# Attention maxima without two small VectorE operations, and every head's first weight tile in float32

## The chip, the cores and the metric

The kernel runs on one core of one Trainium2 chip. The metric is the device time of one execution in microseconds (us). Shown are the median of three runs, and one profiled execution from which all rows come.

## The reference, cut to what matters

Causal attention with a decay bias, then a mixture of experts, then a gated convolution block. Only attention is touched by the change.

```python
def _attn_ref(q, k, v, s):            # q, k, v: 4 x 8 x 576 x 64; s: 4 x 8 x 576
    scores = scale * np.matmul(q, k.transpose(0, 1, 3, 2))
    cum = np.cumsum(np.maximum(s, 0.0), axis=-1)
    bias = -(cum[:, :, :, None] - cum[:, :, None, :])
    scores = np.where(causal, -1e9, scores + np.minimum(bias, 0.0))
    scores = scores - np.max(scores, axis=-1, keepdims=True)
    attn = np.exp(scores)
    attn = attn / (np.sum(attn, axis=-1, keepdims=True) + 1e-09)
    return np.matmul(attn, v)
```

## The kernel before

**Units and steps.** The 32 pairs of batch and head are worked in 8 units of 4 heads. A sequence of 576 is four blocks of 128 positions and a tail of 64; the tails of two heads share one tile. A unit has 14 steps, one score tile each: per pair of heads (0,0), (0,1), (0,2), (1,0), (1,1), (1,2), (1,3), as (head, g). Tile g = 0 has the 512 scores of the head's key block 0 with its four query blocks; the others have the rest of the triangle and the tails. All engines work in the order in which the program is written, so the order is set by the loop over steps and by tables of step numbers (`PAR`).

**One step** (the loop at the end of `attention`) writes, in this order: the maxima's reductions that the step before left (`am`); the planned work of the step; the score products of this tile (`scores`, L443, L446, L471, into `z`, three PSUM buffers); up to two pieces of the *next* unit's maxima products (`stage_a`, L335, into `za`, two PSUM buffers), whose reductions go on VectorE at the start of the next step; the exponentials of the tile one step back (`weights`, ScalarE); `rest` of the tile two steps back; and, when a head's last tile is four steps back, its products with v (`values`, L515), then the normalization.

**Maxima.** The row maxima of a unit must be known before its scores are used, since they enter as a row of the score product. `stage_a` makes 14 pieces. Pieces 0 to 10 are the blocks of 128 queries. `last(r)`, r = 0 and 1, has the tails of two heads against 512 keys, and `lastd` the tails against the tails, with the mask. Each piece ends in a VectorE `tensor_reduce` (L338) into columns of `mx` (float32, 128 x 20): 0 to 15 the blocks, 16 and 17 `last`, 18 and 19 `lastd`. Then `max_cols`, two small VectorE operations: the larger of columns 16, 17 and 18, 19 (L398), and all 18 columns scaled by 2^-12 into float16 (L401). `max_turn` transposes these on TensorE by a product with a float16 identity (L411, into `mt`), `max_out` copies the result to SBUF on ScalarE (L416), and `max_row` writes it into the unit's key tile by DMA. For unit 0 the same is done in three parts (L404, L406).

**Precision of the weights.** The products with v need more than float16. `mode(x)` gives each tile (unit, head, g) with g < 3 a letter from `PAR['m']`, a string of three letters a head:

- `a`: ScalarE writes the exponential twice, as float16 `phi` (L487) and as float32 in place in PSUM (L488); VectorE subtracts the two into float16 `plo` (L499). The score buffer is free after that. `values` makes three float16 products of 65 columns with v's two halves.
- `b`: as `a`, but the float32 copy goes to SBUF (`p`) and GpSimd subtracts (units 0 to 2 use `a` in its place).
- `f`: ScalarE writes the exponential once, as float32 in SBUF (L482), and the score buffer is free. `values` makes one float32 product with the float32 `v0`, which the trace shows as two matmul rows.

Before, the string is `baa baa faa aaa`: only head 2's first tile is in float32. A head has four products with its tile g = 0, one for each query block.

**Behind attention** come the routing (a chain of small operations), the experts, fed by weight loads through a ring of buffers, and the convolution block.

Of the kernel before, what the change touches and what calls it, by code (L numbers as in the profile page):

```python
# [10 lines left out]
F16 = mybir.dt.float16  # L11
I32 = mybir.dt.int32
AF = mybir.ActivationFunctionType
ALU = mybir.AluOpType
# [6 lines left out]
NT = B * S  # L21
# [17 lines left out]
def bc(ap, shape):  # L39
    return ap.to_broadcast(shape)  # L40


class Keep:
# [45 lines left out]
           'pb': 0.377,  # L89
           'c2': 1.0,  # L90
           'pt': 1.003,
           'mct': 1.1,
           'sv0': 1.103,
           'T10': 1.106,
           'mtt': 1.203,
# [8 lines left out]
           'z': 5.0,  # L104
           'lv1': 5.997},
 'r': {'cut': 12, 'w1': 6, 'w2': 8, 'w3': 22},
 'm': 'baabaafaaaaa'}


BEGIN = ([(0, 0), (0, 1), (1, 0), (1, 1), (0, 2), (1, 2), (1, 3)],  # L110
# [3 lines left out]
def attention(tc, ctx, q, k, v, s, xd, rt, hook):  # L114
# [22 lines left out]
    hlp = pool("hl", 1, **right).tile([128, 2, 16, 2, 64], F16, name="h")  # L137
    cum = pool("cum", 1, on=tctx, side="right")

    zero = const.tile([128, 256], F16, name="zero")  # L140
    ident = const.tile([128, 128], F32, name="ident")
    id16 = const.tile([128, 128], F16, name="id16")
    identm = const.tile([128, 128], F16, name="identm")
# [7 lines left out]
    U = {}  # L151
# [171 lines left out]
    mxs = {}  # L323

    def stage_a(u, halves=False):

        mx = mxs[u] = wk.tile([128, 20], F32, name="mx")
        def mcol(i, hs):
            c = 8 * (i % 2) + i // 2 + 2 * hs[0]
            return mx[:, c:c + 2 * len(hs) - 1:2]  # L330

        t, tt = U[u, 1][0:70], T1[0:70]

        def mm(out, l, r, start, stop=False):
            PE.matmul(out, lhsT=l, rhs=r, start=start, stop=stop, skip_group_check=True)  # L335

        def rowmax(out, z, m):
            return lambda: V.tensor_reduce(out, z.rearrange("p (e c) -> p e c", e=m), axis=AX.X, op=ALU.max)  # L338

        def piece(i, hs):  # L340

            n, m = 128 * i + 128, len(hs)
            z = aps.tile([128, 512], F32, name="za")
            for x, h in enumerate(hs):
                y, l = z[:, x * n:x * n + n], block(t, 1, h, i)
                k = whole(t, 0, h)
                if i == 1:
                    mm(y, l, k[:, :, 0:128], x == 0)
                elif i == 3:
                    mm(y, l, k, x == 0)  # L350
                else:
                    mm(y[:, 0:128 * i // 2 + 128], l, k[:, 0, 0:128 * i // 2 + 128], x == 0)
                    if i == 2:
                        mm(y[:, 256:384], l, block(t, 0, h, 1), False)
            for x, h in enumerate(hs):
                c = x * n + (0, 128, 128, 384)[i]
                mm(z[:, c:c + 128], identm, triq, False, True)
            return rowmax(mcol(i, hs), z[:, 0:m * n], m)

        def last(r):  # L360
            z = aps.tile([128, 512], F32, name="za")
            for e in range(2):
                mm(z[64 * e:64 * e + 64], tail(tt, 1, u, 2 * r + e), whole(t, 0, 2 * r + e), True, True)
            return rowmax(mx[:, 16 + r:17 + r], z, 1)

        def lastd(rs):
            z = aps.tile([128, 512], F32, name="za")
            for x, r in enumerate(rs):
                for e in range(2):
                    mm(z[64 * e:64 * e + 64, 64 * x:64 * x + 64], tail(tt, 1, u, 2 * r + e), tail(tt, 0, u, 2 * r + e), x == 0)  # L370
            for x in range(len(rs)):
                mm(z[:, 64 * x:64 * x + 64], identm, tailq, False, True)
            m = len(rs)
            return rowmax(mx[:, 18 + rs[0]:18 + rs[0] + m], z[:, 0:64 * m], m)

        P = []
        if halves:
            for h in (0, 2):
                P += [lambda h=h: piece(0, (h, h + 1)), lambda h=h: piece(1, (h, h + 1))]
                P += [lambda h=h, e=e, i=i: piece(i, (h + e,)) for i in (2, 3) for e in range(2)]  # L380
        else:
            P.append(lambda: piece(0, (0, 1, 2, 3)))
            P += [lambda h=h: piece(1, (h, h + 1)) for h in (0, 2)]
            P += [lambda h=h, i=i: piece(i, (h,)) for i in (2, 3) for h in range(4)]
        P += [lambda r=r: last(r) for r in range(2)] + [lambda: lastd((0, 1))]
        return P


    def key(hs):
        return hs.start if hs else 16  # L390
# [1 line left out]
    def span(hs, tails):  # L392
        return slice(0 if hs else 16, 18 if tails else 8)

    def max_cols(u, hs=slice(0, 4), tails=True):
        mx = mxs[u]
        if tails:
            V.tensor_tensor(mx[:, 16:18], mx[:, 16:18], mx[:, 18:20], op=ALU.max)  # L398
        m = U[u, "16", key(hs)] = wk.tile([128, 18], F16, name="m16")
        if hs == slice(0, 4):  # L400
            V.tensor_scalar(m, mx[:, 0:18], 2.0 ** -12, None, op0=ALU.mult)  # L401
        elif hs:
            i = lambda x: x[:, 0:16].rearrange("p (e h c) -> p e h c", e=2, c=2)[:, :, hs]
            V.tensor_scalar(m[:, 0:8].rearrange("p (e h c) -> p e h c", e=2, c=2), i(mx), 2.0 ** -12, None, op0=ALU.mult)  # L404
        else:
            V.tensor_scalar(m[:, 16:18], mx[:, 16:18], 2.0 ** -12, None, op0=ALU.mult)  # L406

    def max_turn(u, hs=slice(0, 4), tails=True):
        t = U[u, "mt"] = mps.tile([128, 512], F32, name="mt")
        r = span(hs, tails)  # L410
        PE.matmul(t[0:r.stop - r.start, 0:128], lhsT=U[u, "16", key(hs)][:, 0:r.stop - r.start] if key(hs) != 16 else U[u, "16", 16][:, 16:18], rhs=id16, start=True, stop=True, skip_group_check=True)  # L411

    def max_out(u, hs=slice(0, 4), tails=True):
        n = span(hs, tails).stop - span(hs, tails).start
        mr = U[u, "mr", key(hs)] = wk.tile([18, 128], F16, name="mr")
        A.activation(mr[0:n], U[u, "mt"][0:n, 0:128], AF.Copy)  # L416

    def max_row(u, hs=slice(0, 4), tails=True):
        n = 0
# [193 lines left out]
    def plan(t, f):  # L613
        todo.setdefault(math.floor(t), []).append((t, len(todo), f))
# [8 lines left out]
    def begin_a():  # L623
        P0.extend(stage_a(0, True))
        for f in P0[0:6]:
            f()()
        max_cols(0, first, False)

    def second_a():
        for f in P0[6:12]:  # L630
            f()()
        max_cols(0, second, False)

    begin_tasks = dict(
        lk1=lambda: load(1, "k"), lq1=lambda: load(1, "q"), st=lambda: (split_tail("k"), split_tail("q")), tt=turn_tail, ct=copy_tail,
# [1 line left out]
        pa=begin_a, sk1=lambda: split_qk(1, "k"), sq1=lambda: split_qk(1, "q"), mt0a=lambda: max_turn(0, first, False), mo0a=lambda: max_out(0, first, False),  # L637
        mr0a=lambda: max_row(0, first, False), T10=lambda: turn(1, 0), T11=lambda: turn(1, 1), x1=lambda: extra(1),
        pb=second_a, sv0=lambda: split_v(0), lk2=lambda: load(2, "k"), lq2=lambda: load(2, "q"),
        pt=lambda: [P0[12 + i]()() for i in range(3)], mct=lambda: max_cols(0, None), mtt=lambda: max_turn(0, None), mot=lambda: max_out(0, None), mrt=lambda: max_row(0, None),  # L640
        mtb=lambda: max_turn(0, second, False), mob=lambda: max_out(0, second, False), mrb=lambda: max_row(0, second, False),
        z=lambda: Q.dma_start(xd[NT:NT + 128].rearrange("p (j c) -> p j c", c=256), bc(zero[:, None], [128, 4, 256])))
    for n, t in PAR["start"].items():
        plan(t, begin_tasks[n])
    seq = []
# [7 lines left out]
    for u in range(1, NU):  # L653
# [13 lines left out]
        plan(t0 + c["sv"], lambda u=u: split_v(u))  # L667
        for i in range(14):
            pieces.setdefault(t0 + c["pa"] + i * c["pn"] // 14, []).append((u, i))
        plan(t0 + c["mx"], lambda u=u: max_cols(u))  # L670
        plan(t0 + c["mx"] + 1, lambda u=u: max_turn(u))
        plan(t0 + c["mx"] + 1, lambda u=u: max_out(u))
        plan(t0 + c["mx"] + 2, lambda u=u: max_row(u))
# [859 lines left out]
```

## Time and profile before

| | before |
|---|---|
| median of 3 runs | 726.82 us (725.09 to 727.28) |
| profiled execution | 730.22 us, span 728.5 us, mean granted TensorE clock 0.948 |
| attention, about 20 to 250 us | TensorE, VectorE and ScalarE all at work, GpSimd partly |
| routing, about 250 to 275 us | VectorE busy, TensorE at half clock for part of it |
| experts, to about 500 us | DMA and TensorE |
| convolution block, to the end | TensorE |

The busy time of an engine counts its own instructions; matmuls overlap one another, and their ends are modelled, so TensorE's busy time is more than its work. A wait is named by the engine and line that waited, and by what ended it. The clock of a stretch is TensorE's granted share of 2.4 GHz; the engine has two levels, 1.2 and 2.4 GHz, so a mean of 0.93 says that for 14% of the stretch it ran at the lower one.

### The profile page before, as it was taken

Reading aid. Unit: us, or ns where it says so; the run is one execution under the profiler, and the core shown is the slowest. Engines: PE = TensorE matmul, PEld = TensorE weight load, DVE = VectorE, ACT = ScalarE, POOL = GpSimd, SP = SyncE. Lnnn points to the kernel's source line nnn. Section 1 sums busy time; section 2 is a strip of 40 time slices with the busy share of each in tenths; the row PEclk is TensorE's granted clock in tenths of the full one; section 3 lists DMA queues with packets and bytes.
Section 4 is the critical chain, followed back from the end, with each engine's and each line's share of the span. In section 5 each row is a group of like instructions: output and inputs, shape, how many; then the busy total and the mean of one; then the engine's idle time right before and its main releaser. Section 6 shows DMA issues by size and latency. Waiting matters only on the chain. (4 is left out here: it accounts for less than half of the span.)

```text
span 728.5 us, 15503 instructions
## 1 busy us (share of the span) xinstructions
PE 630.6 (87%) x5173; PEld 388.2 (53%) x5173; DVE 463.1 (64%) x868; ACT 399.3 (55%) x674; POOL 263.6 (36%) x372
## 2 busy tenths in 40 slices
PE   0467798898899747799999899999789999999997
PEld 0245676686677633344444344444357766665443
DVE  4775798988885779565594858664119996455000
ACT  4154777887687876354662746443119975445110
POOL 9435767468435019933244345432200000000000
PEclk9999788999898959899999899999999999999999
DMA  9977584784557416899899997965166200000111
GB/s 182 180 147 137 89 150 108 154 161 63 129 186 249 125 25 171 264 264 269 259 313 247 268 271 184 266 145 103 49 129 115 36 16 16 30 23 21 58 44 58
DMA packets 175582, 103.92 MB, mean 143 GB/s; under 512 B 128150, under 2 KB 153534, under 8 KB 175486
## 3 DMA queue, kind: packets, MB, share of 16 engines
q1 hardware_dynamic: 170878, 89.70, 52.3%
q0 software_dynamic: 4272, 12.93, 5.9%
q8 instruction: 47, 0.77, 0.4%
q14 instruction: 49, 0.40, 0.2%
q10 hardware_dynamic: 336, 0.11, 0.1%
HBM read 62.20 MB, written 15.31 MB: 106 GB/s over the span
## 5 line engine op out<-in xcount | busy, mean ns | idle before, releaser
L1143 PE MATMUL hp<-r,xt 128*128 x504 | 116.6, 390 | 9.4 <-ACT xt L1174 8.6
L1143 PE MATMUL yp<-r,ht 128*128 x504 | 112.2, 379 | 1.7 <-PEq L1250 1.7
L1341 PE MATMUL hp<-yt,wi 128*128 128x288 f16 x768 | 95.6, 286 | 2.8 <-DMA yt<-yd 2.8
L1389 PE MATMUL o<-wo,g 128*128 128x512 f16 x432 | 94.5, 379 | 0.0
L1143 PEld LDWEIGHTS <-xt 128*128 128x128 f16 x504 | 50.4, 100 | 72.0 <-ACT xt L1174 9.4
L1341 PEld LDWEIGHTS <-wi 128*128 128x128 f16 x768 | 75.1, 98 | 23.7 <-DMA yt<-yd 3.1
L487 ACT ACTIVATE phi<-z,lnes 128x512 f16<-128x512 f32 (+1 forms) x104 | 67.4, 648 | 24.5 <-PE z L446 23.9
L338 DVE TENSOR_REDUCE mx<-za 128x1 f32<-128x512 f32 (+4 forms) x113 | 67.7, 613 | 19.4 <-PE za L335 18.5
L1143 PEld LDWEIGHTS <-ht 128*128 128x128 f16 x504 | 48.5, 98 | 57.4 <-issue 1.8
L1099 DVE SCALAR_TENSOR_TENSOR r<-st,r 128x512 f32 (+3 forms) x80 | 70.8, 951 | 6.1 <-ACT r L1088 4.4
L1204 POOL DMA_INDIRECT yd<-ys,idx x21 | 22.4, 1066 | 128.9 <-DVEq L1127 81.1
L1389 PEld LDWEIGHTS <-g 128*128 128x128 f16 x432 | 42.3, 98 | 49.5
L1088 ACT ACTIVATE r<-st 128x512 f32 (+3 forms) x84 | 57.1, 764 | 20.8 <-SPq L1136 18.5
L443 PE MATMUL z<-k 71*128 71x256 f16 (+2 forms) x320 | 58.2, 311 | 11.1 <-DVE plo L499 6.0
L499 DVE TENSOR_TENSOR plo<-z,phi 128x512 f16<-128x512 f32 (+1 forms) x94 | 57.6, 614 | 8.5 <-ACT z L488 7.0
L335 PE MATMUL za<-k 70*128 70x256 f16 (+2 forms) x160 | 39.4, 329 | 25.8 <-DMA k<-ex 21.2
L488 ACT ACTIVATE z<-z,lnes 128x512 f32<-128x512 f32 (+1 forms) x94 | 57.9, 616 | 0.0
L1358 DVE SCALAR_TENSOR_TENSOR c<-hb,cw,c 128x576 f32<-128x576 f32 x32 | 26.1, 815 | 35.4 <-ACT c L1352 35.4
L515 PE MATMUL o<-vv,phi 128*128 128x65 f16 (+1 forms) x704 | 47.7, 206 | 0.0
L515 PEld LDWEIGHTS <-phi 128*128 128x128 f16 x736 | 46.2, 104 | 2.1 <-issue 1.2
L515 PE MATMUL o<-vv,plo 128*128 128x65 f16 (+1 forms) x352 | 46.1, 204 | 0.0
L1392 ACT ACTIVATE s<-o 128x512 f32<-128x512 f32 x18 | 10.8, 598 | 63.1 <-PE o L1389 63.1
(274 smaller groups left out, 1100.3 us busy)
## 6 DMA issues: line engine op xcount, KB each, us to landing
st<-in_moe_w_dram SPq DMA_DIRECT2D x8, 2048.0 KB
st<-in_moe_w_dram SPq DMA_DIRECT2D x24, 512.0 KB
out_dram<-s SPq DMA_DIRECT2D x18, 256.0 KB
st<-in_k_dram SPq DMA_DIRECT2D x16, 256.0 KB
st<-in_q_dram SPq DMA_DIRECT2D x16, 256.0 KB
xd<-xh SPq DMA_DIRECT2D x16, 256.0 KB
k<-in_moe_w_dram SPq DMA_DIRECT2D x8, 512.0 KB
s<-in_moe_w_in_dram SPq DMA_DIRECT2D x16, 256.0 KB
```

The costliest lines, as they stand in the source:

```text
L335: PE.matmul(out, lhsT=l, rhs=r, start=start, stop=stop, skip_group_check=True)
L338: return lambda: V.tensor_reduce(out, z.rearrange("p (e c) -> p e c", e=m), axis=AX.X, op=ALU.max)
L443: PE.matmul(out, lhsT=ks[i], rhs=qs[i], start=first and not i, stop=False, skip_group_check=True)
L487: A.activation(hi[:, 0:n], z[:, 0:n], AF.Exp, bias=lnes, scale=1.0 / SC)
L488: A.activation(p[:, 0:n], z[:, 0:n], AF.Exp, bias=lnes, scale=1.0 / SC)
L499: (V if md == "a" else G).tensor_tensor(lo[:, 0:n], p[:, 0:n], hi[:, 0:n], op=ALU.subtract)
L515: PE.matmul(out, lhsT=w, rhs=x, start=first, stop=last, skip_group_check=True)
L1088: i = self.nc.scalar.activation(hi, src, AF.Copy, scale=self.scale[w])
L1099: i = nc.vector.scalar_tensor_tensor(lo, in0=src, scalar=sc, in1=hi, op0=ALU.mult, op1=ALU.subtract)
L1143: i = self.nc.tensor.matmul(out, lhsT=lhsT, rhs=self.rings[w][:, c, k, bass.ds(s, 1), f], **kw)
L1341: PE.matmul(st[x][:, n, 0:HN], lhsT=wi[:, c, k, m], rhs=t[:, n, a + k], start=k + a + c == 0, stop=k == 3 and a == 4)
L1389: PE.matmul(o, lhsT=g[:, a, k, 128 * i:128 * i + 128], rhs=wo[:, c, k], start=j == 0, stop=j == 23)
```

## The change

1. `max_cols` is gone. The scaling by 2^-12 moves into ScalarE's copy behind the turn, and the turn is a float32 product of `mx` itself with the float32 identity.
2. `lastd` comes ahead of the two `last`. Each `last` ends in a `tensor_tensor_reduce`: it adds the float16 `zero` to the PSUM tile in place, and takes the running maximum, which begins with the diagonal's column of `mx`; so the larger of the two needs no operation of its own. It is built as two VectorE instructions, one over 512 columns and one that writes a single column. `zero` grows to 512 columns.
3. For unit 0, whose maxima are turned in halves, the columns of `mx` are laid out so that each half is contiguous.
4. `PAR['m']` becomes `faa faa faa faa`: heads 0, 1 and 3 take `f` for their first tile too, in all eight units.

```diff
-           'mct': 1.1,
...
- 'm': 'baabaafaaaaa'}
+ 'm': 'faafaafaafaa'}
...
-    zero = const.tile([128, 256], F16, name="zero")
+    zero = const.tile([128, 512], F16, name="zero")
...
         def mcol(i, hs):
-            c = 8 * (i % 2) + i // 2 + 2 * hs[0]
+            c = 8 * (hs[0] // 2) + 4 * (i % 2) + i // 2 + 2 * (hs[0] % 2) if halves else 8 * (i % 2) + i // 2 + 2 * hs[0]
...
         def last(r):
...
-            return rowmax(mx[:, 16 + r:17 + r], z, 1)
+            return lambda: V.tensor_tensor_reduce(z, z, zero, 1.0, mx[:, 18 + r:19 + r], ALU.add, ALU.max, mx[:, 16 + r:17 + r])
...
-        P += [lambda r=r: last(r) for r in range(2)] + [lambda: lastd((0, 1))]
+        P += [lambda: lastd((0, 1))] + [lambda r=r: last(r) for r in range(2)]
...
-    def max_cols(u, hs=slice(0, 4), tails=True):
-        mx = mxs[u]
-        if tails:
-            V.tensor_tensor(mx[:, 16:18], mx[:, 16:18], mx[:, 18:20], op=ALU.max)
-        m = U[u, "16", key(hs)] = wk.tile([128, 18], F16, name="m16")
-        if hs == slice(0, 4):
-            V.tensor_scalar(m, mx[:, 0:18], 2.0 ** -12, None, op0=ALU.mult)
...
     def max_turn(u, hs=slice(0, 4), tails=True):
...
-        PE.matmul(t[0:r.stop - r.start, 0:128], lhsT=U[u, "16", key(hs)][:, 0:r.stop - r.start] if key(hs) != 16 else U[u, "16", 16][:, 16:18], rhs=id16, start=True, stop=True, skip_group_check=True)
+        x = mxs[u][:, 0:18] if hs == slice(0, 4) else mxs[u][:, 16:18]
+        if hs and not tails:
+            x = mxs[u][:, 4 * hs.start:4 * hs.stop]
+        PE.matmul(t[0:r.stop - r.start, 0:128], lhsT=x, rhs=ident, start=True, stop=True, skip_group_check=True)
...
-        A.activation(mr[0:n], U[u, "mt"][0:n, 0:128], AF.Copy)
+        A.activation(mr[0:n], U[u, "mt"][0:n, 0:128], AF.Copy, scale=2.0 ** -12)
...
-        plan(t0 + c["mx"], lambda u=u: max_cols(u))
```

VectorE, from the end of a later unit's maxima to the first `plo` behind the turn that needs them (`za` are maxima tiles, `z` score tiles). Before:

```order
L338 TENSOR_REDUCE mx<-za 128x1
L559 TENSOR_TENSOR x<-o,rc 128x4x64
L563 TENSOR_SCALAR xt<-o,rc 64x64 x2
L338 TENSOR_REDUCE mx<-za 128x1
L499 TENSOR_TENSOR plo<-z,phi 128x512
L268 COPY k_138<-k_2461 64x2x1024
L338 TENSOR_REDUCE mx<-za 128x2
L398 TENSOR_TENSOR mx<-mx 128x2
L401 TENSOR_SCALAR m_2829<-mx 128x18
L499 TENSOR_TENSOR plo<-z,phi 128x512
```

And with the change:

```order
L337 TENSOR_REDUCE mx<-za 128x2
L548 TENSOR_TENSOR x<-o,rc 128x4x64
L552 TENSOR_SCALAR xt<-o,rc 64x64 x2
L363 ISA za,mx<-za,zero,mx 128x512
L363 ISA mx 128x1
L488 TENSOR_TENSOR plo<-z,phi 128x512
L267 COPY k_138<-k_2319 64x2x1024
L363 ISA za,mx<-za,zero,mx 128x512
L363 ISA mx 128x1
L488 TENSOR_TENSOR plo<-z,phi 128x512
```

The diagonal's reduction now stands where the first tail's stood, and the last thing ahead of the turn is a tail's reduction of two instructions in place of the diagonal's and the two small ones.

TensorE, the start of head 0's products with v, shortly ahead of the turn. Before:

```order
L335 MATMUL za<-tailq,identm 128x64
L515 LDWEIGHTS phi
L515 MATMUL o<-vv,phi 128x65
L515 LDWEIGHTS phi
L515 MATMUL o<-vv,phi 128x65
L515 LDWEIGHTS plo
L515 MATMUL o<-vv,plo 128x65
```

And with the change:

```order
L334 MATMUL za<-k_139,t_141 64x512
L504 MATMUL o<-v_1830,p_1920 128x65 x2
L504 LDWEIGHTS phi
L504 MATMUL o<-vv,phi 128x65
L504 LDWEIGHTS phi
L504 MATMUL o<-vv,phi 128x65
L504 LDWEIGHTS plo
L504 MATMUL o<-vv,plo 128x65
```

Two float32 products (their weight loads aren't listed apart) stand in place of the first two groups of three float16 products; ahead of them the last maxima tile is now a tail's, of 512 columns, and no longer the diagonal's.

## Rows read from the trace of the kernel before

**Rows 1.** Stretches: us; each engine's busy us (instructions); TensorE's clock; DMA share; GB/s.

```profile
75.00:250.00 175.00, 152.04 (x2336) 125.26 (x2334) 141.79 (x340) 136.74 (x258) 100.81 (x159) 0.89 0.62 142
...
163.00:167.00 4.00, 3.67 (x69) 2.60 (x67) 3.83 (x10) 4.00 (x9) 3.82 (x4) 1.00 0.42 121
...
170.30:173.70 3.40, 3.40 (x28) 2.87 (x26) 1.56 (x4) 2.67 (x6) 3.01 (x2) 0.50 0.04 9
225.00:250.00 25.00, 22.66 (x423) 20.32 (x421) 16.14 (x51) 21.96 (x42) 4.79 (x5) 0.93 0.65 215
```

**Rows 2.** Waits of TensorE in 75 to 250 us: total us, times, longest.

```profile
PE mt L411 <- DVE m L401: 8.6, 6, 1.8
PE z L443 <- DVE plo L499: 8.4, 21, 1.0
```

**Rows 3.** Timeline of VectorE ahead of one turn: start us, us, instruction.

```profile
165.84 0.69 DVE L499 TENSOR_TENSOR plo<-z,phi 128x512 f16<-128x512 f32 x1
...
167.25 0.27 DVE L338 TENSOR_REDUCE mx<-za 128x2 f32<-128x128 f32 x1
167.55 0.80 DVE L398 TENSOR_TENSOR mx<-mx 128x2 f32<-128x2 f32 x1
168.38 0.61 DVE L401 TENSOR_SCALAR m<-mx 128x18 f16<-128x18 f32 x1
```

**Rows 4.** Timeline of TensorE around the same turn; idle time before it in brackets.

```profile
166.59 0.60 PE L443 MATMUL z<-k 71*128 71x512 f16 x2 [0.33 <-DVE plo L499]
167.02 0.22 PE L446 MATMUL z<-trik,identm 128*128 128x128 f16 x1
169.05 0.22 PE L411 MATMUL mt<-id,m 128*18 128x128 f16 x1 [1.81 <-DVE m L401]
169.64 0.57 PE L443 MATMUL z<-k 71*128 71x128 f16 x5 [0.37 <-DVE plo L499]
```

**Rows 5.** Timeline of SyncE's DMA issues, 269 to 280 us.

```profile
273.14 5.86 SPq L1107 DMA_DIRECT2D st<-in_moe_w_dram  x4
```

**Rows 6.** Groups by shape in 75 to 250 us: busy us, mean ns; idle before.

```profile
L487 ACT ACTIVATE phi<-z,lnes 128x512 f16<-128x512 f32 x77 | 53.6, 696 | 19.1 <-PE z L446 18.5
L499 DVE TENSOR_TENSOR plo<-z,phi 128x512 f16<-128x512 f32 x67 | 45.8, 684 | 7.5 <-ACT z L488 6.3 <-issue 0.6
...
L338 DVE TENSOR_REDUCE mx<-za 128x1 f32<-128x512 f32 x36 | 24.2, 679 | 2.1 <-PE za L335 1.8
...
L499 POOL TENSOR_TENSOR plo<-p,phi 128x512 f16<-128x512 f32 x10 | 11.6, 1156 | 14.5 <-ACT p L488 12.5 <-PE za L335 2.0
...
L398 DVE TENSOR_TENSOR mx<-mx 128x2 f32<-128x2 f32 x6 | 6.5, 1084 | 0.2
```

**Rows 7.** Groups by shape over the whole span, of VectorE.

```profile
L1189 DVE SCALAR_TENSOR_TENSOR hs<-hp,hs 128x512 f16<-128x512 f32 x42 | 27.2, 684 | 5.8 <-ACT hs L1188 5.4 <-DVEq L1127 0.2
...
L553 DVE TENSOR_SCALAR rc<-o 128x4 f32<-128x4 f32 x16 | 2.4, 152 | 1.9 <-PE o L515 1.9
...
L401 DVE TENSOR_SCALAR m<-mx 128x18 f16<-128x18 f32 x7 | 2.3, 332 | 0.2
```

**Rows 8.** Instructions on the tile mx: count, shortest/median/longest ns, first and last start.

```profile
L398 DVE TENSOR_TENSOR mx<-mx x8: 160/795/2074, 39.6 to 217.4; 128x2 f32<-128x2 f32 x8
```

**Rows 9.** Timeline of TensorE, head 2's products with v in one unit.

```profile
154.62 0.61 PE L515 MATMUL o<-v,p 128*128 128x65 f32 x4
155.06 0.23 PE L515 MATMUL o<-vv,phi 128*128 128x65 f16 x2
...
155.16 0.41 PE L515 MATMUL o<-v,p 128*128 128x65 f32 x2
155.41 0.23 PE L515 MATMUL o<-vv,phi 128*128 128x65 f16 x2
...
155.50 0.23 PE L515 MATMUL o<-vv,phi 128*128 128x65 f16 x2
```

**Rows 10.** Timeline of VectorE, first copy of the third unit's keys; idle time before it.

```profile
69.44 0.69 DVE L268 COPY k<-k 64x2048 f16<-64x2048 f16 x1 [4.99 <-DMA k<-h]
```

More of the change, by code (lines that the diff above doesn't have):

```diff
@@ L393, in span @@
         return slice(0 if hs else 16, 18 if tails else 8)
-    def max_cols(u, hs=slice(0, 4), tails=True):
-        mx = mxs[u]
-        if tails:
-            V.tensor_tensor(mx[:, 16:18], mx[:, 16:18], mx[:, 18:20], op=ALU.max)
-        m = U[u, "16", key(hs)] = wk.tile([128, 18], F16, name="m16")
-        if hs == slice(0, 4):
-            V.tensor_scalar(m, mx[:, 0:18], 2.0 ** -12, None, op0=ALU.mult)
[L402 to L406, printed above, removed]
     def max_turn(u, hs=slice(0, 4), tails=True):
@@ L626, in begin_a @@
             f()()
-        max_cols(0, first, False)
     def second_a():
@@ L631, in second_a @@
             f()()
-        max_cols(0, second, False)
     begin_tasks = dict(
@@ L639, in attention @@
         pb=second_a, sv0=lambda: split_v(0), lk2=lambda: load(2, "k"), lq2=lambda: load(2, "q"),
-        pt=lambda: [P0[12 + i]()() for i in range(3)], mct=lambda: max_cols(0, None), mtt=lambda: max_turn(0, None), mot=lambda: max_out(0, None), mrt=lambda: max_row(0, None),
+        pt=lambda: [P0[12 + i]()() for i in range(3)], mtt=lambda: max_turn(0, None), mot=lambda: max_out(0, None), mrt=lambda: max_row(0, None),
         mtb=lambda: max_turn(0, second, False), mob=lambda: max_out(0, second, False), mrb=lambda: max_row(0, second, False),
-        z=lambda: Q.dma_start(xd[NT:NT + 128].rearrange("p (j c) -> p j c", c=256), bc(zero[:, None], [128, 4, 256])))
+        z=lambda: Q.dma_start(xd[NT:NT + 128].rearrange("p (j c) -> p j c", c=256), bc(zero[:, None, 0:256], [128, 4, 256])))
     for n, t in PAR["start"].items():
```

## The prediction

> **What bounds the kernel now.** I read the busy line of the page, then the stretches, then who waits for whom, then one unit on its own. In the attention part three engines are nearly full at once [rows 1]: in 75 to 250 us TensorE is busy 152.04 of 175 us, VectorE 141.79, ScalarE 136.74. A busy TensorE there isn't TensorE at its peak: its mean clock in that stretch is 0.89, and as it has only two levels, 22% of 175 us, some 38 us, ran at half speed. One such stretch is in the same group: 170.30 to 173.70, clock 0.50.
>
> The waits say what TensorE lacks most [rows 2]: VectorE's maxima (8.6 us in six waits at L411) and VectorE's `plo` (8.4 us in 21 waits, for a score buffer that isn't free yet). Both end at VectorE. I then followed one maxima turn on both engines [rows 3, 4]. TensorE has finished its scores by 167.24, and its next instruction in order, the turn, starts at 169.05, because VectorE is still at work: `plo`, a copy, the tail diagonal's reduction and the two small operations fill it from 165.84 to 168.99. 1.25 us after the turn starts the clock falls to half [rows 1]. So a turn costs TensorE its wait, and the wait comes before a stretch at half speed.
>
> What follows attention starts when attention ends: the weight loads for the second half are issued at 273.14 [rows 5], behind the routing. I count a microsecond won in attention as one of the total.
>
> **Part 1, the two small operations and the tails' reductions.** Before, the last things VectorE does ahead of a turn are `last(0)`, `last(1)`, the diagonal's reduction and the two small ones: 0.69 + 0.69 + 0.27 + 1.08 + 0.33 us, where the last two are the means of L398 [rows 6] and L401 [rows 7]. The sum is 3.06 us. Now the diagonal comes first (0.27), and each `last` is one operation over 512 columns and one over a single column. The trace of before shows neither. Nearest to the wide one is L1189, which also takes one PSUM and one SBUF tensor through 512 columns: 0.684 us [rows 7]. I take 0.69; below, nothing can go under the 512-column reduction it replaces (0.679 in [rows 6]); above, I allow twice 0.684, since it also writes its sums back to PSUM and keeps a running maximum. Nearest to the narrow one is L553, 0.152 us [rows 7]; I take 0.15, and bound it by 0 and 0.33. New sum: 0.27 + 2 x 0.84 = 1.95 us, so VectorE is ready 1.1 us earlier at each turn.
>
> That L398 works on two columns and still takes 0.160 to 2.074 us [rows 8] means it is held up by something; both its inputs are in SBUF. If the new wide operation could be held up in the same way, by the 0.92 us between L398's mean and its least, the 14 of units 1 to 7 would add 13 us of VectorE time. Its only SBUF tensor is `zero`, and L1189 with one SBUF tensor shows a mean of 0.684, so I count nothing. The Trainium skill (SBUF — State Buffer, "Who interferes with whom") has a rule for this: a VectorE instruction with two SBUF inputs is blocked by a GpSimd instruction that reads SBUF, one with at most one SBUF input isn't. By that rule the sum stays as I have it; without it the 13 us would have to stand in it.
>
> **Part 2, three more heads in float32.** From one piece of the value products [rows 9]: two float32 products take from 154.62 to 155.06, 0.22 each; one between float16 products takes from 155.16 to 155.41, 0.25; a float16 triple that does the same work takes 0.09 (155.41 to 155.50). A head has four such products, two adjacent and two single: 0.94 instead of 0.37 us, **+0.57 us** of TensorE for each head that changes. 24 heads change (three in each of eight units): +13.7 us at full clock. In return ScalarE loses an exponential of 0.70 us per head, and VectorE 14 subtractions of 0.68 (heads 0 and 1 in units 0 to 2, head 3 in all), GpSimd ten of 1.16 (heads 0 and 1 in units 3 to 7) [rows 6]. A score buffer is then free after one exponential instead of an exponential and a subtraction.
>
> Where do the 0.57 us lie? The products of head 3 (of the unit before) and head 0 run in the 9 us ahead of a turn, in which VectorE is the late one. There TensorE comes 1.15 us later to a wait of 8.6 / 6 = 1.43 us [rows 2], and VectorE is 1.1 us earlier: what is left to win is between 1.43 - 1.15 = 0.28 and 1.1; I take 0.5, since the 0.33 us ahead of L443 [rows 4] shrink as well. Six turns: **-3.0 us**. Late next, behind the turn, is the score buffer (0.37 in [rows 4]), so I do not take more. Head 1's 0.57 meets the waits for `plo`: 8.4 us over seven units is 1.2 us a unit. ScalarE and VectorE are each an operation ahead there; I set gain against cost: 0.
>
> **Part 3, the float32 turn.** The matrix has 18 columns of weights and streams 128 columns, against 65 in [rows 9], where each of a product's two instructions takes 0.11 us. By the columns that is 0.22 to 0.44 us in place of one float16 product, so at most +0.4, once a unit. It lies ahead of the score buffer's wait [rows 4], which covers it: 0. Without that cover it is up to +3 us over eight units.
>
> **Part 4, the clock.** 38 us at half speed cost at most 19 us. With shorter waits at the turns some of these stretches should not begin. I take a quarter: **-4.8 us**; bounds 0 and -12.7 (rival B).
>
> **Part 5, the ends.** In unit 0 VectorE loses two 512-column subtractions (1.4 us) ahead of 55 us; but the copy of the third unit's keys then waits 4.99 us for a DMA [rows 10], whose landing follows only as far as ScalarE's splits come earlier. I take **-1.0**, between 0 and -1.4. In the last unit (225 to 250) VectorE has little to do and ScalarE is busy 21.96 of 25 [rows 1]: 3 x 0.70 fewer there against 3 x 0.57 more on TensorE: 0. GpSimd's ten subtractions and the wider memset of `zero` (once, at the start) are covered: GpSimd is busy 100.81 of 175 us [rows 1].
>
> **Sum.** -3.0 - 4.8 - 1.0 = -8.8 us. The profiled execution took 730.22 us (span 728.5), 3.40 above the median of 726.82; its sum is 721.4, and against the median **718.0 us**.
>
> **The rivals.** *A, TensorE becomes the bound, slower:* the 13.7 us fall due in full, since nothing in 163 to 167 us leaves TensorE room (3.67 of 4.00 busy) [rows 1]. The waits at the turns go (-8.6), the clock stays: +5.1, 732 us. It decides from the point at which the removed waits are less than what the products add, 1.72 us a unit. For it speaks that full stretch; against it that the waits of [rows 2] alone are 17.0 us, beside the 19 us lost at half speed. *B, the clock comes back:* if two thirds of the time at half speed vanish, 12.7 of the 19 us are won instead of 4.8: 710 us. The Trainium skill (TensorE: Matmul & The Clock Gate, "Part 1: The HAM clock gate") says that idleness sets the lower rate and sustained work lifts it; by that rule, removing the wait removes the stretch. The trace agrees for one turn [rows 1, 4]; no row shows a turn without a wait. *C, the new reduction costs twice:* 16 x 0.68 = 10.9 us more on VectorE, just ahead of the turns, which eats parts 1 and 4 (7.8 us), while the rest lies beside TensorE's longer products: 726 us. The same comes out if the small read waits for the wide operation to drain.
>
> **How the numbers follow.** Forecast 0.50 (its own range 713 to 724), A 0.17, B 0.23, C 0.10. A measurement here tells some 0.3%, 2.2 us, from no change. Faster: 0.47 of the forecast, all of B, 0.01 of C: 0.71. Same: 0.03 + 0.04 of A + 0.07 of C: 0.14. Slower: 0.13 of A + 0.02 of C: 0.15. The range, 707 to 730, leaves out the slower half of A and B's far end.
>
> **What would show it.** Right: TensorE's wait at the turn under 0.7 us; the wide operation near 0.69 and the narrow near 0.15; float32 products at 0.94 us a head; clock in attention above 0.92; fewer waits for `plo`. Wrong: no waits and a longer unit (A), the clock at 0.98 (B), the wide operation over 1 us (C).

## The result, and the profile after

In one comparison on one chip, eight runs of each, the kernel before took a median of 728.66 us (725.09 to 732.29) and the changed kernel 720.88 us (718.04 to 723.06). The ratio is **0.9896**, with a 95% interval of 0.9866 to 0.9926: 7.6 us won, between 5.4 and 9.8. Here and below, executions over 1.5% longer than the fastest of their kernel count in the medians, but not in the ratios and means. The profiled execution after took 722.48 us, span 720.8, mean granted clock 0.942 (before: 730.22, 728.5, 0.948).

Where the 7.7 us between the two spans came from is read off three starting times. The third unit's turn didn't move: 70.57 us before, 71.19 after. The last turn came at 219.45 before and 214.3 after, 5.1 us earlier. The expert weights' first loads were issued at 273.14 before [rows 5], and now at 266.22 (the same view, SyncE's DMA issues of the kernel after), 6.9 us earlier:

```profile
266.22 5.85 SPq L1093 DMA_DIRECT2D st<-in_moe_w_dram  x4
```

So the gain arose between the third unit and the end of attention, and 0.8 us lies behind. In the last unit the kernel after was 1.7 us shorter from its turn to the end of its normalization; single executions differ by up to 4 us there among kernels that are alike in it, so I draw nothing from that.

**TensorE's waits** in 75 to 250 us of the kernel after (total us, times, longest; line numbers are 11 lower than before, L411 is now L400, L338 is L337, L499 is L488, L443 is L432):

```profile
PE za L334 <- DVE mx L337: 7.8, 3, 5.6
PE z L432 <- DVE plo L488: 2.3, 5, 0.8
...
PE mt L400 <- DVE mx L363: 0.6, 2, 0.3
```

Against [rows 2], the waits at the turns went from 8.6 to 0.6 us and those for `plo` from 8.4 to 2.3. One line grew: TensorE's wait for a maxima buffer, L334 now and L335 before, was 3.9 us in a single wait and is now 7.8 in three, the longest 5.6. Where it comes from is shown below.

**VectorE before the same turn** as in [rows 3], timeline of the kernel after (start us, us, instruction):

```profile
163.87 0.25 DVE L337 TENSOR_REDUCE mx<-za 128x2 f32<-128x128 f32 x1
...
164.97 0.76 DVE L363 CUSTOM_DVE_ANT_0 za<-za,zero,mx 128x512 f32<-128x512 f32 x1
165.75 0.08 DVE L363 DVE_READ_ACCUMULATOR2_ANT mx<- 128x1 f32 x1
...
167.44 0.74 DVE L363 CUSTOM_DVE_ANT_0 za<-za,zero,mx 128x512 f32<-128x512 f32 x1
168.12 0.13 DVE L363 DVE_READ_ACCUMULATOR2_ANT mx<- 128x1 f32 x1
```

**TensorE at that turn**, same kernel; idle time would stand in brackets:

```profile
168.46 0.31 PE L435 MATMUL z<-trik,identm 128*128 128x128 f16 x1
168.71 0.61 PE L400 MATMUL mt<-ident,mx 128*18 128x128 f32 x2
169.25 1.03 PE L432 MATMUL z<-k 71*128 71x128 f16 x6
```

VectorE is through at 168.25, TensorE comes to the turn only at 168.71, and there is no bracket. Before, TensorE stood there for 1.81 us [rows 4]. But this turn now lies in a stretch at half speed (163.2 to 173.4, below), which makes TensorE late as well. The turn of the unit before it runs at full clock and shows the change itself:

```profile
142.70 0.38 PE L400 MATMUL mt<-ident,mx 128*18 128x128 f32 x2 [0.30 <-DVE mx L363]
```

Here VectorE is still the later of the two, by 0.30 us; the same unit's turn waited 1.19 us in the kernel before (at 144.81). Of the six turns in 75 to 250 us, two have a wait, 0.6 us together.

**Stretches** of the kernel after (columns as in [rows 1]):

```profile
75.00:250.00 175.00, 160.12 (x2308) 136.33 (x2306) 130.69 (x340) 130.10 (x245) 88.59 (x149) 0.93 0.64 149
...
125.00:150.00 25.00, 24.63 (x388) 21.42 (x387) 21.10 (x60) 19.94 (x37) 15.33 (x20) 1.00 0.75 144
150.00:175.00 25.00, 22.61 (x266) 18.25 (x263) 17.81 (x42) 17.68 (x34) 14.41 (x19) 0.80 0.50 104
...
47.10:71.00 23.90, 20.89 (x143) 15.82 (x143) 15.72 (x30) 8.66 (x14) 16.02 (x22) 0.50 0.72 153
88.10:101.80 13.70, 11.03 (x73) 7.77 (x73) 9.19 (x18) 4.45 (x8) 8.48 (x34) 0.50 0.67 168
163.20:173.40 10.20, 9.95 (x68) 7.34 (x67) 7.59 (x20) 4.63 (x10) 4.44 (x4) 0.50 0.24 70
```

TensorE is busy 160.12 of 175 us instead of 152.04, VectorE 130.69 instead of 141.79, ScalarE 130.10 instead of 136.74. The mean clock there is 0.93 instead of 0.89, and the half-speed stretches lie elsewhere. Before, there were eight around these 175 us (3.4 to 7 us each), five of them beginning right behind a turn. None of these five is left, and 125 to 150 us is whole at 1.00; but there are long ones elsewhere: 47.1 to 71.0, 88.1 to 101.8, 163.2 to 173.4.

**The new limit.** In front of the last two of these, VectorE stands at a copy of turned keys (L267) until their transpose has landed, and TensorE stands behind VectorE. Timeline of VectorE, then of TensorE, kernel after:

```profile
89.25 0.69 DVE L267 COPY k<-k 64x2048 f16<-64x2048 f16 x1 [4.00 <-DMA k<-st]
...
161.04 1.30 DVE L267 COPY k<-k 64x2048 f16<-64x2048 f16 x1 [3.73 <-DMA k<-h]
```

```profile
90.71 0.32 PE L334 MATMUL za<-t 70*64 70x64 f16 x4 [5.62 <-DVE mx L337]
...
162.99 0.48 PE L334 MATMUL za<-k,t 70*64 70x512 f16 x2 [2.00 <-DVE mx L337]
```

The same two kinds of wait were 1.0 and 0.5 us before (2.9 and 1.1 in the other profiled execution of that kernel). For the copy at 161.04 the DMA isn't later: SyncE issued the transposes at 151.53 us (151.06 before), and before, VectorE began this copy at 161.21 without a wait. VectorE came to it earlier. For the copy at 89.25 it is both: VectorE was free for it at 85.25 instead of 87.01, and the transposes, issued at 79.21 instead of 78.43, landed 1.2 us later. Through its reductions, which are queued behind the copy, it holds up TensorE's maxima buffers, and then the clock falls: at 163.20, right behind the 2.00 us wait.

### The profile page after: what moved, and what is told of

Its sections match the earlier page's. It is cut to its first block, busy times and chain, and to the rows that moved or that the text cites. A ratio compares the mean times of both kernels' runs of the same rounds, so it can differ in the third digit from the quotient of the medians.

```text
span 720.8 us, 15276 instructions
## 1 busy us (share of the span) xinstructions
PE 639.1 (89%) x5087; PEld 399.5 (55%) x5087; DVE 446.1 (62%) x852; ACT 385.8 (54%) x650; POOL 251.7 (35%) x362
## 5 line engine op out<-in xcount | busy, mean ns | idle before, releaser
L1129 PE MATMUL hp<-r,xt 128*128 x504 | 114.1, 383 | 10.2 <-ACT xt L1160 7.1
L337 DVE TENSOR_REDUCE mx<-za 128x1 f32<-128x384 f32 (+4 forms) x97 | 56.9, 602 | 17.4 <-PE za L334 16.7
L476 ACT ACTIVATE phi<-z,lnes 128x512 f16<-128x512 f32 (+1 forms) x80 | 50.1, 627 | 29.3 <-PE z L435 29.2
L432 PE MATMUL z<-k 71*128 71x256 f16 (+2 forms) x320 | 55.4, 301 | 6.7 <-DMA k<-mr 4.2
L334 PE MATMUL za<-k 70*128 70x256 f16 (+2 forms) x160 | 37.4, 314 | 26.8 <-DMA k<-ex 20.8
L488 DVE TENSOR_TENSOR plo<-z,phi 128x512 f16<-128x512 f32 (+1 forms) x80 | 48.2, 603 | 12.1 <-ACT z L477 11.5
L504 PE MATMUL o<-v,p 128*128 128x65 f32 x256 | 48.1, 301 | 0.0
L477 ACT ACTIVATE z<-z,lnes 128x512 f32<-128x512 f32 (+1 forms) x80 | 47.9, 598 | 0.0
L504 PE MATMUL o<-vv,phi 128*128 128x65 f16 (+1 forms) x512 | 43.7, 207 | 0.0
L504 PEld LDWEIGHTS <-phi 128*128 128x128 f16 x544 | 43.5, 112 | 0.0
```

What stands on the lines that cost most here:

```text
L432: PE.matmul(out, lhsT=ks[i], rhs=qs[i], start=first and not i, stop=False, skip_group_check=True)
L476: A.activation(hi[:, 0:n], z[:, 0:n], AF.Exp, bias=lnes, scale=1.0 / SC)
L477: A.activation(p[:, 0:n], z[:, 0:n], AF.Exp, bias=lnes, scale=1.0 / SC)
L488: (V if md == "a" else G).tensor_tensor(lo[:, 0:n], p[:, 0:n], hi[:, 0:n], op=ALU.subtract)
L504: PE.matmul(out, lhsT=w, rhs=x, start=first, stop=last, skip_group_check=True)
L1129: i = self.nc.tensor.matmul(out, lhsT=lhsT, rhs=self.rings[w][:, c, k, bass.ds(s, 1), f], **kw)
```

## The experiments

The kernel before ran beside them in three comparisons: medians of 726.98, 729.37 and 728.14 us. Ratios are to the kernel before on the same chip. Three kernels (the two that fill the turns, and the one that fills them and copies later) compute products that nobody reads; all others do the work of the reference and no more.

### The kernel before once more

Edit: none.

> The kernel before, unchanged, as one of the kernels compared: tells how far two equal kernels stand apart in such a comparison. Theory: 1.000, between 0.997 and 1.003. Rival (the gains of 1% are partly the comparison's own): 0.993 or less, or 1.007 or more.

Measured: **0.9976** (0.9935 to 1.0017). Equal kernels stood 0.24% apart, with the interval over 1. The gains of 1% are not the comparison's own, but two kernels that differ by 0.3% aren't told apart below.

### Maxima alone, and the float32 heads alone

Edits, each from the changed kernel back or from the kernel before forward:

```diff
 # maxima alone: the changed kernel, with
- 'm': 'faafaafaafaa'}
+ 'm': 'baabaafaaaaa'}
 # float32 heads alone: the kernel before, with
- 'm': 'baabaafaaaaa'}
+ 'm': 'faafaafaafaa'}
```

> The change without the three more heads in float32 (the string of modes as before); maxima without the two small operations. My theory (the two parts each give about half; the waits at the turns are won by the maxima, and TensorE's longer products are paid from waits that the released score buffers save): 3 to 5 us faster than before, TensorE's wait at the turns under 0.5 us a unit, waits for plo still about 8 us in 75 to 250 us. Rival one (the whole gain is the maxima's, the float32 heads only cost): 9 us or more faster, that is faster than the full change. Rival two (the gain is the float32 heads'): within 2 us of before.

Measured: 717.45 us, **0.9898** (0.9857 to 0.9939). TensorE's waits in 75 to 250 us:

```profile
PE z L432 <- DVE plo L488: 6.3, 17, 1.0
...
PE mt L400 <- DVE mx L363: 1.8, 3, 0.9
```

> The kernel before with only the string of modes changed: every head's first tile in float32, the two small operations kept. My theory: 2 to 5 us faster than before, the turns still wait about 1 us for VectorE. Rival one (these heads only cost TensorE 13.7 us, partly hidden): 3 us or more slower. Rival two (they carry the gain): 7 us or more faster, as the full change.

Measured: 725.01 us, **0.9991** (0.9961 to 1.0021). TensorE's waits in 75 to 250 us of the kernel with the float32 heads alone:

```profile
PE mt L411 <- DVE m L401: 5.4, 5, 1.6
PE z L443 <- DVE plo L499: 3.5, 8, 0.8
```

My theory, about half the gain from each part, is wrong: the maxima carry all of it, and the heads nothing that can be measured, alone or on top (0.9896 with them, 0.9898 without; these two come from different comparisons, and their difference is known to some 0.5%). The rival that wanted 9 us or more from the maxima alone was too high too; they gave 7.4 us. With the heads alone, TensorE's waits shrink from 8.6 + 8.4 to 5.4 + 3.5 us [rows 2], 8.1 us, and the time stays. The float32 products fill these waits instead of removing them. The waits for `plo` are the heads' doing: 3.5 us with the heads alone, but 6.3, and one more of 3.8 at another line, with the maxima alone.

### The float32 turn alone, and the joined tails alone

Edits, both to the kernel before. The first takes away L401 (the scaling) in units 1 to 7 and keeps L398. The second takes away L398 and keeps the scaling and the float16 turn.

```diff
 # float32 turn alone
-    V.tensor_scalar(m, mx[:, 0:18], 2.0 ** -12, None, op0=ALU.mult)
+    PE.matmul(t[0:18, 0:128], lhsT=mxs[u][:, 0:18], rhs=ident, ...)
...
 # joined tails alone
-            return rowmax(mx[:, 16 + r:17 + r], z, 1)
+            return lambda: V.tensor_tensor_reduce(z, z, zero, 1.0, mx[:, 18 + r:19 + r], ALU.add, ALU.max, mx[:, 16 + r:17 + r])
...
-            V.tensor_tensor(mx[:, 16:18], mx[:, 16:18], mx[:, 18:20], op=ALU.max)
```

> The kernel before, and in units 1 to 7 only the second of the two small operations taken away: the turn is a float32 product of the maxima, ScalarE scales behind it; the larger of tails and diagonal is still VectorE's two-column operation, the diagonal comes last, and the modes are as before. Theory (most of the wait was that first operation, 1.08 us against 0.33): 1 to 3 us faster than before, turns still waiting about 1 us. Rival (any shortening of the wait is enough to keep the clock): 6 us or more faster. Other rival (the float32 turn costs what it saves): within 1 us of before.

Measured: 719.47 us, **0.9902** (0.9869 to 0.9936): more than the theory's 1 to 3 us, and as much as its first rival asked. Waits at the turns in 75 to 250 us:

```profile
PE mt L412 <- DVE mx L398: 6.7, 6, 1.6
```

> The kernel before, with the tails' maxima begun from the diagonal's and the 1.08 us operation of L398 gone; the float16 scaling of L401 and the float16 turn stay. VectorE has 1.08 - 2 x (0.754 + 0.133 - 0.69) = 0.69 us less ahead of a turn. Theory (what counts is that VectorE comes earlier to the turn, by whatever way): waits at the turns fall from 8.6 us to about 4 to 5, and the time to 0.988 to 0.994 of the kernel before, like the float32 turn alone (0.990). Rival (the turn itself, which reads float32 maxima with no scaling in between, is what pays): 0.997 to 1.003.

Measured: 721.15 us, **0.9907** (0.9868 to 0.9947). Waits in the same stretch:

```profile
PE z L441 <- DVE plo L497: 7.7, 21, 1.0
PE mt L409 <- DVE m L399: 6.3, 5, 1.5
```

Either half of the maxima part gives what both give. The waits at the turns fell by only 1.9 and 2.3 us in these profiles, to more than the 4 to 5 us that I had expected of the joined tails. The two operations aren't independent, as their groups in 75 to 250 us show, first of the kernel before, then of the one with joined tails:

```profile
L401 DVE TENSOR_SCALAR m<-mx 128x18 f16<-128x18 f32 x6 | 2.1, 358 | 0.2
...
L399 DVE TENSOR_SCALAR m<-mx 128x18 f16<-128x18 f32 x6 | 3.9, 658 | 0.2
```

With L398 gone, the scaling behind it took 0.30 us longer on average, so 0.69 - 0.30 = 0.39 us a turn was saved, and 6 x 0.39 is the 2.3 us of the waits. It now stands where L398 stood, beside GpSimd's work (Part 1 below). So either shortening of VectorE ahead of the turn pays, it pays more than its own length, and the second pays nothing more that can be measured. Why 0.33 us a turn is worth 7 us in time isn't settled.

### The waits at the turns filled

Edit to the kernel before, in `max_turn`; a second kernel has the same in the changed kernel. Six unread products of 512 columns run ahead of the turns of units 2 to 7, so TensorE works where it used to stand.

```diff
+        if u > 1:
+            for _ in range(6):
+                PE.matmul(t, lhsT=id16, rhs=T2[:, 0, 0], start=True, stop=True, skip_group_check=True)
```

> The kernel before, with six products of 512 columns that nobody reads ahead of each turn of units 2 to 7 (1.3 us at full clock, written to the tile that the turn then overwrites), so that TensorE works where it waited and nothing else changes. Theory (the wait itself brings the half-speed stretch behind it): granted clock in 75 to 250 us up from 0.89 to 0.93 or more and 2 to 6 us faster than before, with the turns still at VectorE's pace. Rival (the half-speed stretches have another cause, or cost nothing as VectorE sets the pace): clock within 0.02 of before, or clock up and the time within 1.5 us of before.

Measured: 716.98 us, **0.9893** (0.9856 to 0.9930). TensorE at the turn of [rows 4] in this kernel, timeline:

```profile
168.45 1.79 PE L413 MATMUL mt<-t,id 128*128 128x512 f16 x6
170.17 0.22 PE L414 MATMUL mt<-id,m 128*18 128x128 f16 x1
170.33 0.63 PE L446 MATMUL z<-k 71*128 71x128 f16 x6
```

The first of the six still run slowly, in a half-speed stretch (162.5 to 169.0) that begins behind a wait of VectorE for a key copy. The whole of 75 to 250 us:

```profile
75.00:250.00 175.00, 152.31 (x2404) 122.70 (x2402) 143.94 (x349) 138.93 (x261) 100.04 (x156) 0.94 0.64 149
```

Nothing was taken from any engine here, and work was added; what changed is that TensorE doesn't stand at the turns (its waits there are 0.7 us). The clock in that stretch rises from 0.89 to 0.94, none of the five half-speed stretches behind a turn is left, and over the timed runs the mean clock is 0.968 instead of 0.955. The gain, 7.8 us, is above the theory's 2 to 6. This shows that the half-speed stretches behind the turns cost about as much as the whole gain of the change. The Trainium skill (TensorE: Matmul & The Clock Gate, "Part 1: The HAM clock gate") says that idleness brings the lower rate; these runs agree, 0.89 with the waits and 0.94 with the same waits filled. VectorE's waits for the key copies are 7.1 us in this execution too, against 1.5 before.

> The full change with the same six unread products of 512 columns ahead of the turns of units 2 to 7 that won 1.1% on the kernel before. Theory (they helped there because TensorE waited there, and here it hardly waits): no gain, between 0 and 8 us slower than the change (1.3 us for each of six turns), ratio to before 0.990 to 1.001. Rival (more work for TensorE lifts the clock whatever else stands): 3 us or more faster than the change, ratio under 0.985.

Measured: 728.32 us, **0.9976** (0.9935 to 1.0017), where the changed kernel stands at 0.9896. In the changed kernel TensorE hardly waits at the turns any more (0.6 us), so the same products only take time.

### The copies later

Edit to the changed kernel: VectorE's copies of the turned keys and queries one or two steps later, for unit 3 also the first maxima piece one step later. The same edit was made to the maxima alone, to the kernel before, and to the kernel before with filled turns.

```diff
- 'u3': {..., 'cp': (-23, -21), 'sv': -1, 'pa': -20, 'pn': 14, 'mx': -6},
+ 'u3': {..., 'cp': (-21, -20), 'sv': -1, 'pa': -19, 'pn': 13, 'mx': -6},
...
-       'cp': (-25, -22),
+       'cp': (-23, -21),
```

> The full change, and the copies of the keys of units 3 and later moved one or two steps later (unit 3's maxima pieces one step later too), so that VectorE doesn't stand at a copy whose transpose hasn't landed. In the changed kernel's trace VectorE stands 4.0 us at 89 us and 3.7 us at 161 us, and both times a stretch at half speed lies around it. Theory (what now ends the gain is VectorE's queue behind these two copies): the two waits go, 4 to 8 us faster than the change, clock in 150 to 175 us back at about 1.00. Rival (the transposes themselves are late for the unit that needs them): the wait moves to the maxima products on TensorE, and the time is within 2 us of the change.

Measured: 715.04 us, **0.9831** (0.9791 to 0.9870). Its stretches, and TensorE's waits in 75 to 250 us:

```profile
75.00:250.00 175.00, 161.89 (x2351) 137.61 (x2348) 132.77 (x355) 133.06 (x251) 88.30 (x149) 0.95 0.66 152
150.00:175.00 25.00, 24.30 (x370) 20.81 (x367) 20.17 (x51) 19.87 (x37) 18.16 (x22) 1.00 0.68 123
```

```profile
PE z L432 <- DVE plo L488: 2.3, 6, 0.8
...
PE za L334 <- DVE mx L337: 1.3, 3, 0.9
```

The row that had grown to 7.8 us is down to 1.3, VectorE has no wait for a key's DMA left in that stretch, and 150 to 175 us, at 0.80 in the changed kernel, is whole at 1.00. By its ratio this is the fastest kernel here.

> The copies moved later, as in the run before, but with the modes as in the kernel before, so without the three more heads in float32. Theory (with the waits at turns and copies gone TensorE sets the pace, and 0.57 us a head is then paid): 3 to 8 us faster than the same with the float32 heads, ratio to before 0.972 to 0.980. Rival (the released score buffers pay for them): within 2 us of it, ratio 0.981 to 0.986. Other rival (VectorE and ScalarE set the pace then): slower than it.

Measured: 715.09 us, **0.9845** (0.9788 to 0.9903). Again with the float32 heads or without them, the time is the same.

> The kernel before with the key and query copies of units 3 to 7 one or two steps later, and nothing else. Theory (the copies stand in the way only once VectorE comes earlier to them): within 0.3% of the kernel before, 0.997 to 1.003. Rival (later copies are worth their 0.65% by themselves): 0.992 to 0.995. A second rival (they push VectorE's work into the turns, where it is late already): 1.004 to 1.010.

Measured: 725.67 us, **0.9959** (0.9918 to 1.0001), between the theory's range and the rival's, and no further from 1 than the unchanged kernel's interval reaches. Its waits tell more:

```profile
PE z L443 <- DVE plo L499: 11.2, 21, 1.5
PE z L443 <- ACT p L482: 4.6, 2, 4.3
PE mt L411 <- DVE m L401: 2.8, 4, 1.6
```

Less at the turns (2.8 instead of 8.6), more for `plo` and ScalarE (15.8 instead of 8.4 + 0.9), and a clock of 0.88 in 75 to 250 us: the waits only moved.

> The kernel before with six unread products of 512 columns on TensorE ahead of the turns of units 2 to 7, and with the later copies. The products alone gave 0.989. Theory (with the clock kept up behind the turns, VectorE comes earlier to the copies there too and waits for their transposes): 0.982 to 0.986, as much more as the later copies gave the change (0.65%). Rival (VectorE is still late at the turns and gains nothing on the transposes): 0.987 to 0.992.

Measured: 716.70 us, **0.9873** (0.9822 to 0.9924), beside 0.9893 without the later copies. Theory and rival can't be told apart by that. In the profile the copies' waits are gone and the clock in 75 to 250 us is 0.96, but TensorE still waits 10.5 us for `plo` (11.4 with the filled turns alone) and 4.6 us for ScalarE's `p` (0.9): part of what the copies free is taken up there.

### The clock, over all timed runs

Every timed run lists its span s and its mean granted clock c. With the two levels, s x (1 - c) is the most that half speed can have cost, and s x c is the rest. Means in us over the runs on which the ratios rest, with the standard error of each mean; the changed kernel's own comparison lists no clocks for the kernel before:

| kernel | runs | time | s x c | s x (1 - c) |
|---|---|---|---|---|
| before, in the three comparisons | 16, 16, 24 | 726.4, 727.4, 727.7 | 692.2, 690.7, 691.2 (0.6 to 0.8) | 32.5, 35.1, 34.8 (0.5 to 0.7) |
| changed | 8 | 720.9 | 686.6 (2.4) | 32.5 (2.6) |
| - its runs with c of 0.959 to 0.964 | 5 | 720.4 | 691.4 | 27.3 |
| - its runs with c of 0.942 to 0.944 | 3 | 721.7 | 678.7 | 41.3 |
| maxima alone | 6 | 718.5 | 684.5 (2.1) | 32.2 (1.3) |
| float32 turn alone | 12 | 720.4 | 687.0 (1.6) | 31.7 (1.6) |
| joined tails alone | 10 | 719.9 | 689.1 (0.9) | 29.1 (1.1) |
| filled turns | 7 | 718.1 | 693.3 (0.9) | 23.1 (0.6) |
| changed, copies later | 6 | 714.8 | 683.0 (2.8) | 30.1 (3.0) |

The kernel with filled turns wins in the last column alone (-9.4 us). For the changed kernel the mean misleads: its runs fall into two groups that lie 14 us apart in the last column and 1.3 us apart in time. The profiled execution is one of the three with the low clock, and its stretch from 47.1 to 71.0 makes 12 us of the last column by itself; that the two others had it too, no trace shows. In the kernel with the later copies, where 25 to 75 us is whole at 1.00, unit 0's last turn and the third unit's lie 27.5 us apart (46.78 to 74.30), against 30.0 in the changed kernel (41.20 to 71.19). So half speed cost some 1 to 3 us there and not 12: the last column is an upper bound, not a price. In the five other runs all of the gain stands in the last column (27.3 against 32.5 to 35.1), in the three none of it. The maxima alone have -7.7 and -0.3 against their comparison's own kernel before, the two half parts some of each. How the changed kernel's 7 us divide between shorter waits and less half speed can't be read from this table.

## Why the prediction was right

**The time and the sign.** 718.0 us was forecast, a gain of 8.8; 7.6 was measured. The cause named, VectorE's last work ahead of the turn, is the one that the experiments found. How the 7.6 us divide among the terms of the sum, the runs don't settle; that it came out so near the total isn't shown to be more than luck.

**Part 1, right.** The reduction's two instructions, by tile, in the kernel after (count, shortest/median/longest ns), with the turn:

```profile
L400 PE MATMUL mt<-ident,mx x20: 269/329/421, 26.0 to 214.4; 128*18 128x128 f32 x14, 128*8 128x128 f32 x4, 128*2 128x128 f32 x2
L363 DVE CUSTOM_DVE_ANT_0 za<-za,zero,mx x16: 729/754/759, 37.9 to 213.1; 128x512 f32<-128x512 f32 x16
L363 DVE DVE_READ_ACCUMULATOR2_ANT mx<- x16: 82/133/143, 38.5 to 213.7; 128x1 f32 x16
```

The wide one is 0.754 us (taken: 0.69), the narrow one 0.133 (0.15). With the diagonal's 0.28, VectorE's work ahead of the turn is 2.05 us (1.95), against 3.06 before. No wide one was held up: the longest of 16 is 0.759, where L398 had reached 2.074 [rows 8]. That settles rival C. The rule of the Trainium skill (SBUF — State Buffer, "Who interferes with whom"), by which an instruction with at most one SBUF input, outside VectorE's 2-port modes, isn't held up by GpSimd, agrees with these 16, nine of which overlap a `tensor_tensor` of GpSimd.

What held L398 up can be read from the timelines of GpSimd and VectorE in the kernel before:

```profile
119.30 2.12 POOL L251 TENSOR_TENSOR st<-st,st 128x1024 f16<-128x1024 f32 x1
119.36 2.07 DVE L398 TENSOR_TENSOR mx<-mx 128x2 f32<-128x2 f32 x1
...
166.87 1.47 POOL L574 TENSOR_TENSOR xh<-x,xh 128x512 f16<-128x512 f32 x1
...
193.65 0.16 DVE L398 TENSOR_TENSOR mx<-mx 128x2 f32<-128x2 f32 x1
```

Three of the eight L398 had no `tensor_tensor` of GpSimd beside them and took 0.16 us. The five others began during one, took 0.80 to 2.07 us, and ended within 0.02 us of its end, as the one at 167.55 [rows 3] does. L399 of the joined tails, with one SBUF input, took 1.71 us beside such an instruction, so one SBUF input alone doesn't spare an operation that wait; which mode it ran in, no run shows.

**Part 2, the price right, the net gain not.** One piece of the value products after, timeline of TensorE; head by head they now look like this:

```profile
140.20 0.66 PE L504 MATMUL o<-v,p 128*128 128x65 f32 x4
140.69 0.23 PE L504 MATMUL o<-vv,phi 128*128 128x65 f16 x2
...
140.78 0.41 PE L504 MATMUL o<-v,p 128*128 128x65 f32 x2
141.03 0.23 PE L504 MATMUL o<-vv,phi 128*128 128x65 f16 x2
...
141.56 0.22 PE L504 MATMUL o<-vv,phi 128*128 128x65 f16 x2
...
141.65 0.23 PE L504 MATMUL o<-vv,phi 128*128 128x65 f16 x2
```

Two adjacent float32 products take 0.49 us (140.20 to 140.69), a single one 0.25, a float16 triple 0.09: 0.99 us a head, 0.94 was taken. The groups of 75 to 250 us shrank as expected:

```profile
L488 DVE TENSOR_TENSOR plo<-z,phi 128x512 f16<-128x512 f32 x56 | 38.3, 685 | 8.2 <-ACT z L477 7.8
...
L476 ACT ACTIVATE phi<-z,lnes 128x512 f16<-128x512 f32 x56 | 38.6, 689 | 22.7 <-PE z L435 22.6
```

That is 11 of VectorE's subtractions and 21 of ScalarE's exponentials fewer than in [rows 6]. The forecast gave the turns, in parts 1 and 2 together, -3.0 us: the wait less what the heads add. The runs don't bear out that subtraction. By the step "What is left to win is between 0.28 and 1.1", taken as 0.5, the heads should have eaten 0.6 us a turn, 3.6 us, of what the maxima win. But the heads alone give 0.9991 (0.9961 to 1.0021), and on top of the maxima 0.9896 beside 0.9898, with the later copies 0.9831 beside 0.9845: their 15 us of products (24 x 0.62) show no cost. As these pairs are known to 0.5 and 0.7%, some 4 to 5 us, a cost of 3.6 us isn't ruled out either. The waits for `plo`, where I had set gain against cost, fell by 6.1 us in the profile, and the runs with one part alone put that down to the heads.

**Part 3, right.** The float32 turn is two rows of 0.269 to 0.421 us, 0.38 together at full clock (142.70); no wait for the score buffer follows it there, and the float32 turn alone made the kernel faster.

**Part 4, the direction right, the size open.** A quarter of 19 us, -4.8, was taken. In the profile the clock of 75 to 250 us did rise to 0.93, as forecast, and the turns' half-speed stretches did go. Against the 32.5 to 35.1 us of the kernel before, s x (1 - c) is 5 to 8 us lower in five of the eight runs and 6 to 9 higher in three, at nearly the same time, so it doesn't give the size. The step overlooked that half speed taken from the turns can come back elsewhere: two stretches behind the key copies, and one at 47.1 to 71.0, where the mean clock of 25 to 75 us fell from 0.96 to 0.76 (at little cost, as the section on the clock shows). That the half-speed time behind the turns is worth much, as rival B had it, is shown by the filled turns, which won 9.4 us of it.

**Part 5, open, small.** In the profile nothing was won at the start: the third unit's turn is at 71.19 us instead of 70.57, and the third unit's copy still waits for its DMA, as [rows 10] had shown. In the two kernels without the added float32 heads this turn comes at 64.95 and 65.58, and in the kernel before once more at 69.68, so one execution doesn't settle 1 us.

**What the sum left out.** It asked "what is late next" only at the turn, where it found the score buffer. What was late next was a DMA: VectorE, ahead of time, ran into the transposes of the next keys, and 7.7 us of its waits stand there in this execution (4.0 with the maxima alone). Moving the copies took the ratio from 0.9896 to 0.9831, some 0.6%, though the intervals touch (0.9866 and 0.9870).

**Rival A** didn't happen: the heads' products weren't paid in full anywhere.

## What to carry to other kernels

When several engines are nearly full and one of them makes TensorE stand at a fixed point of a loop, shortening its work ahead of that point paid once here, whichever operation was taken; look then at what that engine runs into next, and move its work that depends on a DMA later in the same change. Before paying for a shorter wait, fill it with unread products: one cheap run tells how much of the loss is the clock and how much is the wait. Work added to TensorE showed no cost here where it lay in waits that stay, and should be tested apart from the part that removes them.

## What the runs showed of the hardware that I had not expected

- Unread work made the kernel faster: 36 products of 512 columns added, 0.9893 of the time, with the mean granted clock at 0.968 instead of 0.955.
- The reduction with a running maximum takes 0.754 us over 512 columns and its second instruction 0.133, together 0.21 us more than the plain reduction's 0.679, and GpSimd's work beside it doesn't show in it; a two-column `tensor_tensor` with both inputs in SBUF took 0.16 us alone and up to 2.07 beside GpSimd's `tensor_tensor`, ending with it.
- A float32 product of 65 columns takes 0.25 us, nearly three times the 0.09 of the three float16 products that do its work, and 24 heads of them changed no time that can be measured.
- The same key copy (L267, 64 x 2048) took 0.69 us at 89.25 and 1.30 us at 161.04, where a `tensor_tensor` of GpSimd ran until 161.79. That this lengthened it wasn't tried.
- Half speed costs far from the same everywhere: runs of the changed kernel whose granted clock puts 14 us between their bounds, s x (1 - c), lie 1.3 us apart in time.
